# Expert and output products of 512 columns, and the last combine transposes moved into the output phase, in an attention and soft-MoE kernel on one core

## The chip, the cores and the metric

The kernel runs on one core of a Trainium2 chip. The core has a matrix engine (TensorE, PE in the profile), a vector engine (VectorE, DVE), an activation engine (ScalarE, ACT), a general engine (GpSimd, POOL) and a synchronising engine (SyncE, SP), and 16 DMA engines that move data between the chip's memory (HBM) and the on-chip buffer (SBUF). TensorE writes its products to PSUM, a small memory of eight banks; a bank holds 512 float32 columns on 128 partitions. The metric is device time in microseconds (us) of one launch.

## What is computed

The first half is chunk-selected attention. For 4 batches and 8 heads, sequence 768, head size 64, each query keeps 6 of 24 chunks of 32 keys, by an upper bound on the scores, and attends causally inside them. The second half is a soft mixture of experts on the result:

```python
x = attn_out.transpose(0, 2, 1, 3).reshape(B * S, H * D)      # 3072 x 512
logits = x @ phi                                              # 3072 x 32 (8 experts, 4 slots each)
d = np.exp(logits - logits.max(0, keepdims=True))
d /= d.sum(0, keepdims=True) + 1e-09                          # over all 3072 rows
slot_input = (d.T @ x).reshape(E, S_per_e, D)                 # 8 x 4 x 512
for e in range(E):
    h = np.maximum(slot_input[e] @ w1[e], 0.0)                # 512 -> 1024
    slot_out[e] = h @ w2[e]                                   # 1024 -> 512
c = np.exp(logits - logits.max(1, keepdims=True))
c /= c.sum(1, keepdims=True) + 1e-09                          # over the 32 slots of a row
out = c @ slot_out                                            # 3072 x 512
```

The inputs are float32; the loads turn them into bfloat16. The two weight tensors w1 and w2 are 16.8 MB each in float32, the output is 6.3 MB.

## The kernel before, in words

**Attention.** There are 16 steps, one for a pair of heads of one batch (4 steps for a batch). The order of the instructions on each engine is written out by hand. Each step does scores, exponentials, masks and the product with the values for its pair, and parts of the neighbours' work. The loads of k, q, v and of the 16 weight matrices (1 MB each in bfloat16, `load_w`, line 131) are issued by GpSimd, one queue, in a written order; `wplan` (line 518) says in which step a weight is asked for. The last one, the second matrix of the last expert, is asked for at the start of the last step, and its buffer takes the memory of tiles of earlier steps.

**The MoE part, batch by batch.** When a batch's four steps are through, its logits are made (`moe_logits`, line 389), the running column maximum is kept, the exponentials `d_sb` are taken, and `moe_dispatch` (line 478) multiplies them with x into the slot inputs; a fifth group of six products with a matrix of ones gives the column sums. Both are added to `si_acc`, which is rescaled when the maximum grows. `moe_ct` (line 495) transposes the row-wise exponentials `c_pad` of a batch on TensorE, six at a time, and VectorE copies them to `cT_all`.

**The last batch (lines 660 to 768)** does the same on a shorter way. Its logits are multiplied twice: once into `lg1`, from which the maxima are taken, and once into `lg2`, a PSUM tile to which a further product adds the negated maximum (line 720), so that ScalarE's exponential (line 728) reads it directly. `keep` issues unneeded products that keep TensorE busy.

**The experts (lines 771 to 859).** Eight experts with four slots each would leave most of the array empty; four experts are placed side by side, in four groups of 32 columns of the array. `experts_in` multiplies by w1, 512 columns at a time, for two halves f of the hidden size and two groups g of four experts; `relu` and `hidden_T` turn the result. `experts_out` (line 808) multiplies by w2 in two halves y of 256 columns, each in a PSUM tile and bank of its own, for the first seven experts. `last_expert_out(y)` (line 819) does the last expert, eight products for each half. `sums` (line 797) turns the slot sums into `zinv` and the last batch's row sums into `inv_b`, by one reciprocal. Behind the first half ScalarE scales by `zinv` (line 857), behind the second VectorE does (line 859); both write `so_sb`.

**The output (lines 861 to 889).** The 24 blocks of 128 rows go in 12 pairs, m = 0 to 11; a pair is 512 KB. The first pair is made in halves of 256 columns in four PSUM tiles and stored in three pieces (tile `first`). For the others two products of 256 columns fill a block, ScalarE scales the first block of a pair and VectorE the second, and SyncE issues the store (line 889; for the last pair block by block, line 887). There are five SBUF buffers for these pairs, so pair m = 5 waits until the first pair has been stored, and so on. The PSUM tiles come from three pools, `sc` and `tp` with two buffers and `at` with one.

Of the kernel before, what the change touches and what calls it, by code (L numbers as in the profile page):

```python
# [10 lines left out]
F32 = mybir.dt.float32  # L11
BF16 = mybir.dt.bfloat16
# [6 lines left out]
CH = 32  # L19
# [41 lines left out]
def kernel(  # L61
# [416 lines left out]
    def moe_dispatch(b):  # L478
        d_sb = st.pop(("d", b))
        x = st.pop(("x", b)).rearrange("p t h d -> p t (h d)").rearrange("p t (a c x) -> p t a x c", a=NDG // 2, x=2)  # L480
        si = p_tp.tile([P, NDG + 1, NS], F32, name="si_ps", tag="tp")
        for dg in range(NDG + 1):
            for t in range(NQT):
                nc.tensor.matmul(
                    si[:, dg, :], lhsT=x[:, t, dg // 2, dg % 2, :] if dg < NDG else ones_sq,
                    rhs=d_sb[:, t, :], start=(t == 0), stop=(t == NQT - 1),
                )
        if b == 0:
            nc.vector.tensor_copy(si_acc, si)
        elif b < B - 1:  # L490
            nc.vector.tensor_tensor(si_acc, si_acc, si, op=ALU.add)
        else:
            st["si"] = si
# [190 lines left out]
    lg2 = p_sc.tile([P, 2, 512], F32, name="lg2_ps", tag="sc")[:, 0, :NQT * NS].rearrange("p (t s) -> p t s", t=NQT)  # L684
    h_ps = [p_sc.tile([P, 2, 512], F32, name="h_ps0", tag="sc")]
    moe_logits(BL, range(NDG - 1), lg2, False)
# [19 lines left out]
    moe_logits(BL, range(NDG - 1, NDG), lg2, False)  # L706
# [6 lines left out]
    inv_b = tail.tile([P, 1 + NQT], F32, name="inv_b")  # L713

    def cinv(n):
        return inv_a[:, n:n + 1] if n < BL * NQT else inv_b[:, 1 + n - BL * NQT:2 + n - BL * NQT]

    keep(2)
    rep = identf[:NS, :NS].rearrange("p (o s) -> p o s", o=1)
    nc.tensor.matmul(  # L720
        lg2, lhsT=mneg.broadcast_to([NS, P]), rhs=rep.broadcast_to([NS, NQT, NS]), start=False, stop=True,
    )
# [4 lines left out]
    d_sb = small.tile([P, NQT, NS], BF16, name="d_sb", tag="d_sb")  # L727
    nc.scalar.activation(d_sb, lg2, func=ACT.Exp)
    st["d", BL] = d_sb
    rm = small.tile([P, NQT, 1], F32, name="rm", tag="rm")  # L730
    nc.vector.tensor_reduce(rm, lg1, axis=AX.X, op=ALU.max)
    nc.vector.reciprocal(inv_a, csa)
    dm = small.tile([P, 1, NS], F32, name="dm", tag="dm")
    nc.vector.tensor_tensor(dm[:, 0, :], m_old, bc, op=ALU.add)
# [3 lines left out]
    nc.vector.tensor_tensor(si_acc, si_acc, dm.broadcast_to([P, NDG + 1, NS]), op=ALU.mult)  # L738
    for g in range(2):
# [12 lines left out]
    for g in range(2):  # L752
# [4 lines left out]
            si[:, :NDG, sl].rearrange("p a (j s) -> p a j s", j=4), op=ALU.add,  # L757
        )
    for g in range(2):
# [4 lines left out]
            si[:1, NDG, sl].rearrange("p (j s) -> p j s", j=4), op=ALU.add,  # L764
# [3 lines left out]
    zinv = inv_b[:, :1]  # L768
# [3 lines left out]
    so_sb = [tail.tile([P, Dm // 2], BF16, name=f"so_sb{y}") for y in range(2)]  # L772
# [24 lines left out]
    def sums():  # L797
        ps = p_tp.tile([P, 1 + NQT], F32, name="z_ps", tag="tp")
        nc.tensor.matmul(
            ps[:, :1], lhsT=zrow.rearrange("p j s -> p (j s)"), rhs=identf[:1, :1], start=True, stop=True)  # L800
        col_sums(ps[:, 1:], BL)
        nc.vector.reciprocal(inv_b, ps)

    HD = Dm // 2
    so_t = p_at.tile([P, 2, 512], F32, name="so_ps0", tag="at")
    so_ps = [so_t[:, 0, :HD], p_sc.tile([P, HD], F32, name="so_ps1", tag="sc")]

    def experts_out(fs, es, ys):
        for y, f in ((y, f) for y in ys for f in fs):
            for fg in range(f * 4, (f + 1) * 4):  # L810
                for e in es:
                    g, j = divmod(e, 4)
                    nc.tensor.matmul(
                        so_ps[y][j * CH:(j + 1) * CH, :], lhsT=hT_pad[:, fg, e, :],
                        rhs=w_sb[E + e][:, fg * Dm + y * HD:fg * Dm + (y + 1) * HD],
                        start=(g == 0 and fg == 0), stop=False,
                    )

    def last_expert_out(y):
# [100 lines left out]
```

## Time and profile before

| what | value |
|---|---|
| median of 3 runs | 165.73 us (165.38 to 166.21) |
| the profiled execution, its own time | 166.11 us |
| its span, first to last instruction | 164.4 us |
| TensorE busy | 141.0 us (86%), 2541 products |
| VectorE busy | 121.8 us (74%) |
| ScalarE busy | 122.9 us (75%) |
| GpSimd busy | 103.0 us (63%) |
| read from HBM, written | 52.49 MB, 6.29 MB |

The profile shows one execution. A page of it gives the busy time of each engine, the span in 40 slices of 4.11 us, the chain of waits that ended last, the costliest groups of instructions and the DMA issues. Further views list instructions in order of time (timeline), who waited for whom, and the busy time of each engine in chosen windows. A row such as "PE L823 MATMUL so_ps<-w_sb,hT_pad 128*32 128x256 bf16 x16" means: TensorE, line 823, sixteen products into so_ps, each with a stationary operand of 128 by 32 and 256 moving columns. What stands in brackets behind a row is the idle time of the engine before it and what ended that. PEld is TensorE's weight load; SPq is SyncE's queue of issued DMAs.

### The profile page before, as it was taken

Reading aid. Unit: us, or ns where it says so; the run is one execution under the profiler, and the core shown is the slowest. Engines: PE = TensorE matmul, PEld = TensorE weight load, DVE = VectorE, ACT = ScalarE, POOL = GpSimd, SP = SyncE. Lnnn points to the kernel's source line nnn. Section 1 sums busy time; section 2 is a strip of 40 time slices with the busy share of each in tenths; the row PEclk is TensorE's granted clock in tenths of the full one; section 3 lists DMA queues with packets and bytes.
Section 4 is the critical chain, followed back from the end, with each engine's and each line's share of the span. In section 5 each row is a group of like instructions: output and inputs, shape, how many; then the busy total and the mean of one; then the engine's idle time right before and its main releaser. Section 6 shows DMA issues by size and latency. Waiting matters only on the chain.

```text
span 164.4 us, 6143 instructions
## 1 busy us (share of the span) xinstructions
PE 141.0 (86%) x2541; PEld 97.3 (59%) x2541; DVE 121.8 (74%) x424; ACT 122.9 (75%) x168; POOL 103.0 (63%) x203
## 2 busy tenths in 40 slices
PE   7696779999999999999999899998989999494600
PEld 2253356766777686676777567775768748372300
DVE  4466989999999989999997999899526521175530
ACT  3759879999999898999898899997886311183530
POOL 6988759989889398888949896768937100000000
PEclk9999999999999999999999999999999999959755
DMA  3999999999999999999999999999999999159994
GB/s 48 137 134 166 203 184 135 174 191 203 201 201 205 202 204 182 211 196 177 211 189 215 194 213 193 210 219 195 206 209 212 211 217 197 34 198 370 405 408 157
DMA packets 40604, 32.94 MB, mean 200 GB/s; under 512 B 26368, under 2 KB 34816, under 8 KB 40576
## 3 DMA queue, kind: packets, MB, share of 16 engines
q0 software_dynamic: 38416, 26.25, 108.5%
q1 hardware_dynamic: 2160, 6.29, 9.8%
q8 instruction: 20, 0.33, 0.8%
q14 instruction: 8, 0.07, 0.1%
HBM read 52.49 MB, written 6.29 MB: 358 GB/s over the span
## 4 chain that ended last, share of the span: by engine, by line
PE 36%; DMA 24%; ACT 14%; DVE 11%; issue 6%; POOL 4%; DVEq 0%; POOLq 0%; ACTq 0%; SPq 0%
DMA w_sb<-in_moe_w_dram 15%; ACT e_sb L325 10%; PE sc_ps L301 7%; DMA out_dram<-o_sb 6%; PE at_ps L353 6%; PE sc_ps L311 5%; PE tr_ps L209 5%; ACT qT L218 3%; PE xT_ps L375 3%; DMA k_in<-in_k_dram 3%; PE ub_ps L260 2%; DVE x_sb L366 2%; DVE mx L272 2%; DVE qpn L243 1%; PE ub_ps L253 1%
## 5 line engine op out<-in xcount | busy, mean ns | idle before, releaser
L325 ACT ACTIVATE e_sb<-sc_ps 128x1024 bf16<-128x1024 f32 (+1 forms) x96 | 83.2, 917 | 7.7 <-PE sc_ps L311 7.2
L335 POOL TENSOR_SCALAR_AFFINE_SELECT e_sb<-e_sb 128x256 bf16<-128x256 bf16 x96 | 38.4, 418 | 16.2 <-ACT e_sb L325 15.7
L301 PE MATMUL sc_ps<-qT,kT 64*128 64x384 bf16 (+3 forms) x258 | 36.8, 305 | 2.7 <-ACT e_sb L325 1.9
L311 PE MATMUL sc_ps<-nsT,smask 64*128 64x384 bf16 (+2 forms) x294 | 38.2, 284 | 0.1
L353 PE MATMUL at_ps<-v_t,e_sb 128*128 128x65 bf16 x672 | 29.7, 194 | 1.2 <-DVE x_sb L366 1.0
L353 PEld LDWEIGHTS <-e_sb 128*128 128x128 bf16 x672 | 25.5, 98 | 3.5 <-issue 1.9
L301 PEld LDWEIGHTS <-kT 64*128 64x128 bf16 x258 | 14.0, 93 | 10.9 <-issue 5.4
L272 DVE MAX8 mx<-ub_ps 128x8 f32<-128x8 f32 (+1 forms) x192 | 16.8, 162 | 3.8 <-PE ub_ps L260 2.9
L311 PEld LDWEIGHTS <-smask 64*128 64x128 bf16 x294 | 15.0, 94 | 3.8 <-issue 0.6
L151 POOL DMA_DIRECT2D v_t<-in_v_dram x16 | 16.6, 1039 | 0.6 <-PE ns_ps L283 0.5
L227 DVE TENSOR_REDUCE mm<-kT 128x24 bf16<-128x768 bf16 x16 | 15.1, 943 | 2.2 <-ACT kT L218 2.2
L366 DVE TENSOR_TENSOR x_sb<-at_ps,inv 128x768 bf16<-128x768 f32 (+1 forms) x17 | 15.5, 910 | 0.6
L233 DVE TENSOR_REDUCE mm<-kT 128x24 bf16<-128x768 bf16 x16 | 15.1, 942 | 0.0
L218 ACT COPY qT<-tr_ps 128x768 bf16<-128x768 bf16 x16 | 12.8, 799 | 2.3 <-PE tr_ps L209 2.3
L218 ACT COPY kT<-tr_ps 128x768 bf16<-128x768 bf16 x16 | 12.9, 804 | 1.0 <-PE tr_ps L209 1.0
L146 POOL DMA_DIRECT2D k_in<-in_k_dram x16 | 11.7, 734 | 1.1 <-POOLq L904 0.8
L146 POOL DMA_DIRECT2D q_in<-in_q_dram x16 | 11.5, 720 | 0.0
L139 POOL DMA_DIRECT2D w_sb<-in_moe_w_dram x16 | 11.4, 716 | 0.0
L882 PE MATMUL o_ps<-so_sb,cT_all 128*128 128x256 bf16 x44 | 8.0, 332 | 3.7 <-ACT o_sb L844 3.6
L386 DVE COPY xT_sb<-xT_ps 128x768 bf16<-128x768 bf16 (+1 forms) x15 | 8.0, 537 | 3.2 <-PE xT_ps L375 3.2
L209 PE MATMUL tr_ps<-ident,k_in 128*64 128x128 bf16 x192 | 8.4, 223 | 0.9 <-DMA k_in<-in_k_dram 0.8
L247 DVE TENSOR_SCALAR qpn<-qT 128x768 bf16<-128x768 bf16 x15 | 9.1, 607 | 0.0
(131 smaller groups left out, 210.3 us busy)
## 6 DMA issues: line engine op xcount, KB each, us to landing
w_sb<-in_moe_w_dram POOLq DMA_DIRECT2D x16, 1024.0 KB, 13.4
out_dram<-o_sb SPq DMA_DIRECT2D x10, 512.0 KB, 5.2
k_in<-in_k_dram POOLq DMA_DIRECT2D x16, 192.0 KB, 6.8
q_in<-in_q_dram POOLq DMA_DIRECT2D x16, 192.0 KB, 7.1
v_t<-in_v_dram POOLq DMA_DIRECT2D x16, 192.0 KB, 8.4
out_dram<-o_sb SPq DMA_DIRECT2D x2, 256.0 KB, 4.8
out_dram<-first SPq DMA_DIRECT2D x2, 128.0 KB, 2.0
out_dram<-first SPq DMA_DIRECT2D x1, 256.0 KB, 2.3
```

The source lines that it names most:

```text
L146: nc.gpsimd.dma_start(out=t, in_=src.rearrange("h (p g) d -> p h (g d)", p=P))
L151: nc.gpsimd.dma_start(out=v_t[i % NV][:, :, :, :D], in_=v[b, 2 * j:2 * j + 2].rearrange("h (g p) d -> p h g d", p=P),)
L209: nc.tensor.matmul(ps[h * 64:(h + 1) * 64, g, :], lhsT=src[:, h, g * D:(g + 1) * D], rhs=ident, is_transpose=True,)
L218: nc.scalar.copy(t.rearrange("d (p g) -> d p g", g=NQT), st.pop((nm + "ps", i)).rearrange("d g p -> d p g"),)
L227: nc.vector.tensor_reduce(mm[:, 0, 0, :], kT, axis=AX.X, op=ALU.min)
L272: nc.vector.max(mx[:, a, :], ub[:, a, :max(8, 4 * t + 4)])
L301: nc.tensor.matmul(ps[:, h, c:c + w], lhsT=kT[r, kg * P:(kg + 1) * P], rhs=qT[r, qs], start=True, stop=False,)
L311: nc.tensor.matmul(ps[:, h, c + (f - t0) * P:c + (l - t0) * P], lhsT=smask[r, x, kg].rearrange("p a b -> p (a b)"), rhs=nsT[r, (f - x * NJ ...
L325: nc.scalar.activation(e[:, :, :w], st.pop(("scps", i, g))[:, :, :w], func=ACT.Exp, scale=scale)
L335: nc.gpsimd.affine_select(out=e[:, :, c:c + P], in_=e[:, :, c:c + P], compare_op=ALU.is_ge, fill=0.0, base=0, pattern=[[0, 2], [1, P]], ch ...
L353: nc.tensor.matmul(o, lhsT=st["e", i, g][:, h, c:c + P], rhs=v_t[i % NV][:, h, kg, :], start=(kg == 0), stop=(kg == t),)
L366: nc.vector.tensor_tensor(st["x", b][:, t0:t1, 2 * j:2 * j + 2, :].rearrange("p t h d -> p h t d"), at[:, :, :, :D], inv.broadcast_to([P, ...
```

## The change

It has five parts.

1. `moe_dispatch`: the ones product runs once with 192 columns instead of six times with 32; VectorE then sums over the six row blocks (`z`) and adds the sum to `si_acc`.
2. The last batch's logits are made once. VectorE copies the broadcast negated maximum to SBUF (`bc_sb`), adds it to the logits (`ld`), and ScalarE's exponential reads `ld`. The reciprocal of the other batches' row sums moves behind the scaling of `si_acc`.
3. The second expert products go over 512 columns into one PSUM tile `so_ps`; `last_expert_out` runs once, and both halves are scaled behind it, the first by ScalarE and the second by VectorE, into one tile `so_all`.
4. An output block is one product of 512 columns. The order of the PSUM pools changes: ("at", "tp", "sc", "tp", "sc") for ("sc", "tp", "tp", "sc", "at"), and for the first pair ("sc", "sc") for ("sc", "at").
5. `moe_ct` of the last batch, its column sums and their reciprocal leave the expert phase (`last_rows`) and come behind pair m = 3 in the output loop. `slot_sums` keeps the part for `zinv`.

```diff
     def moe_dispatch(b):
...
-        si = p_tp.tile([P, NDG + 1, NS], F32, name="si_ps", tag="tp")
-        for dg in range(NDG + 1):
+        ps = p_tp.tile([P, (NDG + NQT) * NS], F32, name="si_ps", tag="tp")
+        si = ps[:, :NDG * NS].rearrange("p (a s) -> p a s", a=NDG)
+        zt = ps[:, NDG * NS:].rearrange("p (t s) -> p t s", t=NQT)
+        for dg in range(NDG):
...
+        nc.tensor.matmul(zt, lhsT=ones_sq, rhs=d_sb, start=True, stop=True)
...
+        z = small.tile([P, NS], F32, name="z", tag="z")
+        nc.vector.tensor_reduce(z, zt.rearrange("p t s -> p s t"), axis=AX.X, op=ALU.add)
+        if b == 0:
+            nc.vector.tensor_copy(si_acc[:, NDG, :], z)
         else:
-            st["si"] = si
+            nc.vector.tensor_tensor(si_acc[:, NDG, :], si_acc[:, NDG, :], z, op=ALU.add)
...
-    moe_logits(BL, range(NDG - 1), lg2, False)
...
-    moe_logits(BL, range(NDG - 1, NDG), lg2, False)
...
-    nc.tensor.matmul(
-        lg2, lhsT=mneg.broadcast_to([NS, P]), rhs=rep.broadcast_to([NS, NQT, NS]), start=False, stop=True,
-    )
...
-    nc.scalar.activation(d_sb, lg2, func=ACT.Exp)
...
+    nc.vector.tensor_copy(bc_sb[:, 0, :], bc)
+    ld = small.tile([P, NQT, NS], F32, name="ld", tag="ld")
+    nc.vector.tensor_tensor(ld, lg1, bc_sb.broadcast_to([P, NQT, NS]), op=ALU.add)
+    d_sb = small.tile([P, NQT, NS], BF16, name="d_sb", tag="d_sb")
+    nc.scalar.activation(d_sb, ld, func=ACT.Exp)
...
-    def sums():
-        ps = p_tp.tile([P, 1 + NQT], F32, name="z_ps", tag="tp")
-        nc.tensor.matmul(
-            ps[:, :1], lhsT=zrow.rearrange("p j s -> p (j s)"), rhs=identf[:1, :1], start=True, stop=True)
-        col_sums(ps[:, 1:], BL)
-        nc.vector.reciprocal(inv_b, ps)
+    def slot_sums():
+        ps = p_tp.tile([P, 1], F32, name="z_ps", tag="tp")
+        nc.tensor.matmul(ps, lhsT=zrow.rearrange("p j s -> p (j s)"), rhs=identf[:1, :1], start=True, stop=True)
+        nc.vector.reciprocal(zinv, ps)
+
+    def last_rows():
+        moe_ct(BL)
+        ps = p_tp.tile([P, NQT], F32, name="cs_ps", tag="tp")
+        col_sums(ps, BL)
+        nc.vector.reciprocal(inv_b, ps)
...
-    so_t = p_at.tile([P, 2, 512], F32, name="so_ps0", tag="at")
-    so_ps = [so_t[:, 0, :HD], p_sc.tile([P, HD], F32, name="so_ps1", tag="sc")]
+    so_ps = p_at.tile([P, 2, 512], F32, name="so_ps0", tag="at")[:, 0, :]
...
-    moe_ct(B - 1)
...
-    experts_out([0, 1], [4, 5, 6], [0, 1])
-    last_expert_out(0)
-    nc.scalar.activation(so_sb[0], so_ps[0], func=ACT.Copy, scale=zinv)
-    last_expert_out(1)
-    nc.vector.tensor_scalar_mul(so_sb[1], so_ps[1], zinv)
+    experts_out([0, 1], [4, 5, 6])
+    last_expert_out()
+    nc.scalar.activation(so_sb[0], so_ps[:, :HD], func=ACT.Copy, scale=zinv)
+    nc.vector.tensor_scalar_mul(so_sb[1], so_ps[:, HD:], zinv)
...
-            tag = ("sc", "tp", "tp", "sc", "at")[n % 5]
+            tag = ("at", "tp", "sc", "tp", "sc")[n % 5]
             o_ps = homes[tag].tile([P, Dm], F32, name="o_ps", tag=tag)
-            for y in range(2):
-                nc.tensor.matmul(
-                    o_ps[:, y * HD:(y + 1) * HD], lhsT=cT[:, m, x], rhs=so_sb[y], start=True, stop=True)
+            nc.tensor.matmul(o_ps, lhsT=cT[:, m, x], rhs=so_all, start=True, stop=True)
...
         if m < NM - 1:
             nc.sync.dma_start(out=rows(m), in_=o_sb)
+        if m == 3:
+            last_rows()
```

More of the change, by code (lines that the diff above doesn't have):

```diff
@@ L738 @@
     nc.vector.tensor_tensor(si_acc, si_acc, dm.broadcast_to([P, NDG + 1, NS]), op=ALU.mult)
+    nc.vector.reciprocal(inv_a, csa)
     for g in range(2):
@@ L767 @@
         zrow[:, :, 2 * SPE:3 * SPE], zrow[:, 3:4, SPE:2 * SPE].broadcast_to([1, 4, SPE]))
[L768 removed]
     cT = cT_all.rearrange("p (m a) (c x) -> p m x (a c)", a=2, x=2)
     h_sb = tail.tile([P, 2, 512], BF16, name="h_sb")
[L772 removed]
+    so_all = tail.tile([P, Dm], BF16, name="so_all")
+    so_sb = [so_all[:, y * Dm // 2:(y + 1) * Dm // 2] for y in range(2)]
     h_ps.append(p_sc.tile([P, 2, 512], F32, name="h_ps1", tag="sc"))
```

63 lines of the change are left out of this document (32 added, 31 removed).

## The prediction

> **What bounds the kernel now.** I read the page first, for the stages; then the chain of waits from 110 us on; then the rows of the weight loads, the timeline and the windows of the last 24 us.
>
> ```profile
> PEclk9999999999999999999999999999999999959755
> DMA  3999999999999999999999999999999999159994
> GB/s 48 137 134 166 203 184 135 174 191 203 201 201 205 202 204 182 211 196 177 211 189 215 194 213 193 210 219 195 206 209 212 211 217 197 34 198 370 405 408 157
> ```
>
> From the second slice to the 34th the DMA engines are never under nine tenths busy, at 135 to 219 GB/s; then comes one almost empty slice (34 GB/s), then the output at 370 to 408 GB/s. The granted clock falls right behind that hole.
>
> ```profile
> 118.10 24.61 DMA w_sb<-in_moe_w_dram
> ...
> 142.75 0.43 PE so_ps L823 x8
> ...
> 143.73 0.98 PE oh_ps L866 x4
> 144.71 1.29 PE o_ps L882 x6
> ```
>
> The last weight (the last expert's second matrix) is issued at 118.10 and lands 24.61 us later, behind the loads before it. Its landing starts the last chain: eight products, then (with ScalarE's scaling between) the first output products. The rows of that stretch:
>
> ```profile
> 142.75 0.62 PE L823 MATMUL so_ps<-w_sb,hT_pad 128*32 128x256 bf16 x16 [1.87 <-DMA w_sb<-in_moe_w_dram]
> 143.20 0.47 ACT L857 ACTIVATE so_sb<-so_ps,inv_b 128x256 bf16<-128x256 f32 x1 [6.17 <-PE so_ps L823]
> 143.42 0.48 DVE L859 TENSOR_SCALAR so_sb<-so_ps,inv_b 128x256 bf16<-128x256 f32 x1 [5.03 <-PE so_ps L823]
> 144.29 0.42 PE L866 MATMUL oh_ps<-so_sb,cT_all 128*128 128x256 bf16 x1
> 144.50 0.42 PE L882 MATMUL o_ps<-so_sb,cT_all 128*128 128x256 bf16 x1
> 144.53 0.88 DVE L847 TENSOR_SCALAR first<-oh_ps,inv_a 128x256 f32<-128x256 f32 x2 [0.63 <-PE oh_ps L866]
> ```
>
> TensorE had waited 1.87 us for that weight. So what is taken away ahead of 142.75 buys nothing while the landing stays, and what is added there is free up to 1.87 us. From 142.75 on, delay counts in full as long as the stores run back to back afterwards:
>
> ```profile
> 143.79:147.20 3.41, 3.41 (x17) 2.45 (x17) 2.49 (x5) 2.53 (x5) 0.00 (x0) 0.50 0.43 151
> 147.20:150.60 3.40, 2.48 (x19) 1.67 (x18) 2.07 (x4) 1.62 (x3) 0.00 (x0) 1.00 0.92 360
> 150.60:154.00 3.40, 1.19 (x8) 0.78 (x8) 1.84 (x3) 1.73 (x3) 0.00 (x0) 1.00 1.01 402
> ```
>
> The last three columns are granted clock, DMA share and GB/s. From 147.2 the stores run at 360 to 402 GB/s: the rest of the kernel is a fixed number of bytes, moved by whatever delays its start. The granted clock is 0.50 for 3.41 us after the hole.
>
> **The change, part by part.** *Ahead of the landing.*
>
> ```profile
> 126.81 0.60 PE L395 MATMUL lg_ps<-phi_sb,xT_sb 128*128 128x32 bf16 x18
> 128.32 0.36 DVE L705 TENSOR_REDUCE pm<-lgt_ps 128x32 f32<-128x192 f32 x1 [0.34 <-PE lgt_ps L395]
> 129.38 0.59 PE L720 MATMUL lg_ps<-identf,mb 32*128 32x192 f32 x2
> 130.07 0.33 ACT L728 ACTIVATE d_sb<-lg_ps 128x192 bf16<-128x192 f32 x1 [2.59 <-PE lg_ps L720]
> 130.15 0.19 DVE L734 TENSOR_TENSOR dm<-m_run,bc_ps 128x32 f32<-128x32 f32 x1 [0.35 <-PE bc_ps L724]
> 130.25 0.35 DVE L737 TENSOR_TENSOR lc<-lgt_ps,rm 128x192 f32<-128x192 f32 x1
> 131.06 0.30 PE L484 MATMUL si_ps<-d_sb,ones_sq 128*128 128x32 bf16 x6
> 131.73 1.05 PE L779 MATMUL h_ps<-w_sb,siT_pad 128*32 128x512 bf16 x16
> 132.71 0.51 PE L498 MATMUL cT_ps<-ident,c_pad 128*128 128x128 bf16 x6
> 137.85 0.30 PE L692 MATMUL z_ps<-live,cT_all 128*128 128x1 bf16 x6
> 138.08 2.80 PE L813 MATMUL so_ps<-w_sb,hT_pad 128*32 128x256 bf16 x80
> ```
>
> Removed: the second copy of the logits (18 products in 0.60 us here, six more behind the last head, and the 0.59 us product with the negated maximum). In their place VectorE copies the 32 bounds (near the 0.19 us of the add at 130.15) and adds them to 192 columns (0.35 us, as lc). ScalarE's exponential then waits for VectorE instead of TensorE; dm, lc and the scaling of si_acc stand behind the new add on VectorE. The removed products stand ahead of the last head's transposes, which then start some 0.3 us earlier (an estimate: half of the 0.60), the two VectorE steps and their handovers put about 0.4 us back: between 0.3 us earlier and 0.5 later, I take 0.1 later. The slot sums lose five of six weight loads and products (at most 0.30 us) and gain a 192-column product; in the three earlier batches VectorE gains a 192-to-32 reduction and a 128x32 copy or add, about 0.5 us each time (0.36 as the reduction of pm, 0.19 as the small add). The last combine transposes (0.51 us) and their column sums (0.30) leave this stage. The second expert products become 56 with 512 columns for 112 with 256. Eighty of these take 2.80 us, 35 ns each; the 16 of 512 columns at 131.73 take 1.05 us, 66 ns each, about twice as much: no gain, give or take 0.3 us. Together TensorE is through about 0.8 us sooner (0.5 later to 1.5 sooner), and all of it disappears in the wait for the weight, which grows from 1.87 to some 2.7 us. If the cover were gone, the worst end, three times 0.5 on VectorE plus 0.5, would just use it up: 2.0 against 1.87 plus the 0.8 taken away. The load itself gains one wait on TensorE for memory it reuses, the buffers of an earlier step; it is issued 24.6 us ahead behind a full queue, so a delay of microseconds there leaves the landing. Cost: nothing.
>
> *The split of the last expert.* Today ScalarE starts after 8 of the 16 products, at 143.20. With eight of 512 columns there is no first half: the same columns take the same 0.62 us, and ScalarE starts when VectorE does today, 143.42: **+0.22 us**. Bounds: 0, or 0.43 were the products half clocked.
>
> *Two readers of one bank.* so_ps is now one 512-column tile. In the changed program VectorE's scaling waits for ScalarE's alone, though they read different halves. So VectorE starts at 143.42 + 0.47 + 0.05 = 143.94 instead of 143.42 and ends at 144.43. Behind it on VectorE stand the two pieces of `first`, and TensorE waits for it with the second-half products. The first two products start at 143.95 and 144.16 and no longer hold the third up; the third starts at 144.48, the fourth 0.21 later at 144.69, against 144.29 now: **+0.40 us** in all for everything behind, the 0.22 included, and 0.41 for VectorE's first piece (144.53 now, 144.94). Bounds: 0.22, if the halves overlapped after all, and 0.53, if all waited for VectorE.
>
> The Trainium skill ("PSUM — Partial Sum Buffer", section "PSUM bank collisions raise a hardware error") says that ScalarE and VectorE must not read one bank at once even in different columns, and that dependencies are put between them. By that rule the wait can't be scheduled away and the term is 0.40; without it 0.22. The rows at 143.20 and 143.42, which overlap, are of two different banks, so no run here yet shows it.
>
> *Output products of 512 columns.*
>
> ```profile
> L882 PEld LDWEIGHTS <-cT_all x44: 96/98/152, 144.3 to 155.6; 128*128 128x128 bf16 x44
> L882 PE MATMUL o_ps<-so_sb,cT_all x44: 269/273/421, 144.5 to 155.8; 128*128 128x256 bf16 x44
> ```
>
> Six of them took 1.29 us in the chain at half clock, 0.215 each, while the duration of one is 0.42: starts follow the columns, and one product of 512 columns takes as long as two of 256. The weight loads of 0.15 us lie beside that. Nothing from this; the far end, where each of the first blocks saves a weight load, is a rival below.
>
> *The last transposes among the stores.* They come after the fourth pair of row blocks (m = 3).
>
> ```profile
> L506 DVE COPY cT_all<-cT_ps x4: 543/547/558, 62.0 to 133.3; 128x768 bf16<-128x768 bf16 x4
> L802 DVE RECIPROCAL inv_b<-z_ps x1: 205/205/205, 138.2 to 138.2; 128x7 f32<-128x7 f32 x1
> 145.50:146.00 0.50, 0.50 (x5) 0.32 (x4) 0.40 (x1) 0.36 (x1) 0.00 (x0) 0.50 0.78 260
> 147.31 0.75 DVE L847 TENSOR_SCALAR o_sb<-o_ps,inv_a 128x512 f32<-128x512 f32 x1
> 144.65 0.84 SPq L872 DMA_DIRECT2D out_dram<-first  x2
> 148.13 1.51 SPq L889 DMA_DIRECT2D out_dram<-o_sb  x1
> 149.74 0.39 SPq L889 DMA_DIRECT2D out_dram<-o_sb  x1
> ```
>
> VectorE scales m = 3 until 148.06, so 148.46 in the new time; then copies the transposes (0.55), TensorE sums columns (0.30), VectorE inverts (0.20) and scales m = 4 (0.75), with handovers of 0.05 (ScalarE's end at 143.67, TensorE's start at 143.73): m = 4 is ready at 150.46. On TensorE the products of m = 4 stand behind the column sums, on VectorE its scaling behind the reciprocal. Now SyncE issues that store at 149.74, because the store before it kept SyncE for 1.51 us; then at about 150.5. Is that too late? By 150.60 the windows moved 151 x 3.41 + 360 x 3.40 = 1.74 MB of the 2.10 MB issued before m = 4, so these run out near 151.5 now, 151.9 then. From issue to bytes the first store took about 0.9 us (144.65; by 146.00 the half microsecond from 145.5 is 0.78 busy). 150.5 + 0.9 = 151.4: in time by 0.5 us. Cost: nothing, at most 1.26 us (0.55 + 0.30 + 0.20 + 0.20) if the whole insertion shows.
>
> **Sum:** 0 + 0.40 + 0 + 0 = +0.4 us. The profiled execution took 166.11 us (span 164.4 and 1.7 around it): 166.5. It lies 0.38 above the median of 165.73, whose runs spread from 165.38 to 166.21. On the median: **166.1 us**.
>
> **The rivals.**
>
> *Stores run dry (slower).* The mechanism is the insertion at m = 3; it decides once m = 4 is issued later than about 151.0. For it: only 0.5 us of cover, and SyncE's unexplained 1.51 us hold, which could fall on the fourth store instead; half clock would add up to 0.3 us to the transposes and sums. Against: m = 4 was scaled by about 148.8 (148.06 + 0.75) and waited 0.9 us for SyncE today, and the buffers for m = 5 come free as now. Price 0.2 to 1.2 us, say 0.7: 166.8 us.
>
> *A colder clock (slower).* The hole grows from 1.87 to about 2.7 us, and the window 143.79 to 147.20 shows half clock in one piece of 3.41 us after a hole. If such a piece starts before 142.75, the eight products take about 0.43 us longer, but it also ends earlier. Price 0 to 0.43: 166.1 to 166.5 us. The Trainium skill ("TensorE: Matmul & The Clock Gate", Part 1) says that the window is free-running, 3413 ns long, so where it falls differs between runs; by it this case comes and goes from run to run, which three runs of one kernel without a longer hole can't show.
>
> *Hidden (same).* If the stores' end were set by something that doesn't move with their start, as the 1.51 us hold, nothing is lost: 165.7 us. Against it: 360 to 402 GB/s until the end.
>
> *Faster.* If half clock rather than the columns set the pace of the output, each of the first six row blocks would save a weight load (0.15 us at half clock in the trace): 0.4 - 0.9 = -0.5, so 165.2; and with the hole over at full clock a little under 164.9. Against: 0.215 us from start to start is the columns alone.
>
> That the change does not do what it says can be left out: the changed program holds 64 second products and 22 output products of 512 columns.
>
> **How the numbers follow.** Forecast 0.46; stores run dry 0.26; colder clock 0.12; hidden 0.10; faster 0.06. About 0.5% (0.83 us, 164.9 to 166.56) is what a measurement of this kernel can tell from no change. Within it lie the forecast but for 0.02, the hidden case, half of the cold one and none but the smallest starvation: 0.60; above: 0.34; below: 0.06. The range goes from the lowest run with nothing lost, 165.3, to 166.1 with the far end of a starved store, 167.3.
>
> **What would show it.** Right: the wait for the weight at the last expert's products grows beyond 1.87 us while the weight lands at the same time; ScalarE and VectorE scale so_sb one after the other; the first o_sb store is issued 0.4 us later after the landing; DMA share stays at nine tenths or more around 151 us. Wrong: the weight lands at another time, VectorE's scaling overlaps ScalarE's, a hole in the GB/s around 151 us, or a granted clock of 0.50 already at the last expert's products.

## The result, and the profile after

| | before | after |
|---|---|---|
| median of 20 runs each, side by side | 166.42 us (164.84 to 167.59) | 166.95 us (166.10 to 168.43) |
| ratio after / before, 95% interval | | 1.0066 [1.0041, 1.0091] |
| profiled execution, its span | 166.11, 164.4 | 166.54, 164.8 |
| TensorE busy, products | 141.0, 2541 | 140.1, 2408 |

The kernel became slower by 0.66% by the ratio, about 1.1 us. The ratio leaves out runs that are over 1.5% above the fastest of their kernel, and the medians of all 20 differ by only 0.53 us, so the size of the loss is less certain than the interval says. The forecast was +0.4 us, as a difference that could not be told from no change; the interval excludes no change. Run together once more, below, the ratio was 1.0049 [1.0013, 1.0084].

The page of the changed kernel, the rows that were read first before. Each digit is one of 40 slices of 4.12 us:

```profile
PEclk9999999999999999999999999999999969999955
DMA  3999998999999999999999999999999999058994
GB/s 47 148 144 169 209 175 103 182 198 203 201 204 201 203 203 181 211 191 182 214 188 216 188 214 190 215 215 199 203 207 216 212 216 191 18 190 343 406 409 186
```

Two things differ. The granted clock now falls in slice 33 (131.8 to 136.0 us), in the middle of the expert products and ahead of the hole in the transfers, where before it fell behind it. And the output has a weaker slice of its own (343, DMA 8) and a fuller last one (186 for 157).

The chain of waits of the changed kernel, from the last batch's logits on (shortened):

```profile
126.69 0.57 PE lgt_ps L395 x16
...
131.18 0.33 DVE si_acc L746
131.74 0.56 PE h_ps L689 x2
...
133.87 3.85 PE h_ps L790 x47
...
138.06 0.98 PE h_ps L790 x16
139.04 0.86 PE so_ps L826 x16
...
140.56 2.32 PE so_ps L826 x34
143.09 0.68 PE so_ps L835
143.79 0.48 ACT so_all L867
...
146.76 4.70 DMA out_dram<-o_sb
```

What is missing is the 24.61 us line of the last weight's transfer. Before, the chain went through that transfer; now it goes through steps of several engines until 131.7, the reciprocal last among them, and from there to 143.8 through TensorE's own work without a break. The views of TensorE's waits from 139 to 145 us say the same (waiter, releaser, us in all, times, longest). Before:

```profile
PE so_ps L823 <- DMA w_sb<-in_moe_w_dram: 1.9, 1, 1.9
PE oh_ps L866 <- ACT so_sb L857: 0.4, 1, 0.4
```

After:

```profile
PE oh_ps L875 <- ACT so_all L867: 0.6, 1, 0.6
```

The wait that was to grow from 1.87 to 2.7 us is gone. The timeline of the changed kernel shows the end of the expert products, and the scaling behind it:

```profile
142.50 0.39 PE L835 MATMUL so_ps<-w_sb,hT_pad 128*32 128x512 bf16 x1
...
142.92 0.39 PE L826 MATMUL so_ps<-w_sb,hT_pad 128*32 128x512 bf16 x3
143.13 0.60 PE L835 MATMUL so_ps<-w_sb,hT_pad 128*32 128x512 bf16 x6
...
143.79 0.47 ACT L867 ACTIVATE so_all<-so_ps,zinv 128x256 bf16<-128x256 f32 x1 [4.10 <-PE so_ps L835]
144.30 0.48 DVE L868 TENSOR_SCALAR so_all<-so_ps,zinv 128x256 bf16<-128x256 f32 x1 [3.54 <-ACT so_all L867]
```

L835 is the last expert, L826 the others. By the trace the weight lands 23.0 us behind its issue at 118.57, so at 141.56; its last load packet ends at 141.24. The first product that needs it starts only at 142.50, and at 143.13 TensorE is still at other experts' products: the eight end at 143.73. Before, they ended 0.66 us behind the landing (142.71 and 143.37), which would be 142.22 here. So TensorE is **1.5 us late** behind a weight that landed 1.15 us earlier than before; the products end 0.36 us later. Then the two scalings run one behind the other, as forecast.

Where TensorE lost its time, in the timeline of the changed kernel:

```profile
130.66 0.36 ACT L739 ACTIVATE d_sb<-ld 128x192 bf16<-128x192 f32 x1 [2.71 <-DVE ld L737]
...
131.42 0.26 DVE L747 RECIPROCAL inv_a<-h_ps 128x18 f32<-128x18 f32 x1
131.74 0.56 PE L689 MATMUL h_ps<-w_sb,ident 128*128 128x480 bf16 x2 [1.80 <-DVE inv_a L747]
...
132.14 0.76 PE L486 MATMUL si_ps<-d_sb,x_sb 128*128 128x32 bf16 x24
```

The exponentials `d_sb` are ready at 131.02. The slot inputs' products (L486), which need them, start at 132.14: ahead of them in TensorE's order stand two of the unneeded products that keep it busy (`keep`, L689), and those wait 1.80 us for the reciprocal of the other batches' row sums (L747). Both use one PSUM tile: the row sums lie in columns 0 to 17 of half 1 of `h_ps[0]`, the unneeded products go to columns 32 to 511 of the same half. In part 2 of the change this reciprocal moved behind the scaling of `si_acc`. Before, the same products started at 130.46, 0.06 us behind the exponentials' end at 130.40:

```profile
130.04 0.58 PE L678 MATMUL h_ps<-w_sb,ident 128*128 128x480 bf16 x2
130.46 0.76 PE L484 MATMUL si_ps<-d_sb,x_sb 128*128 128x32 bf16 x24
```

Windows of 3.41 us, laid along the edges of the granted clock (us, then busy time of TensorE, its loads, VectorE, ScalarE, GpSimd, then granted clock, DMA share, GB/s), after:

```profile
129.33:132.74 3.41, 1.61 (x30) 1.18 (x29) 1.83 (x8) 1.00 (x5) 0.00 (x0) 1.00 1.05 211
132.74:136.16 3.42, 3.42 (x34) 1.20 (x33) 0.86 (x5) 0.00 (x0) 0.19 (x1) 0.50 1.05 211
```

and before:

```profile
129.33:132.74 3.41, 3.41 (x56) 2.04 (x56) 1.75 (x9) 1.19 (x5) 0.19 (x1) 1.00 1.06 214
132.74:136.16 3.42, 3.42 (x62) 1.78 (x62) 0.85 (x3) 0.60 (x1) 0.00 (x0) 1.00 1.08 218
```

With the wait TensorE is busy for only 1.61 us of the first window, and the next one is granted half the clock: 34 products for 62. The dispatch is 1.7 us later than before. Of this 0.47 us stood there already at the last normalisation of attention (`x_sb`, 126.78 for 126.31) and 0.15 us comes from the new steps to the exponentials; the other 1.1 us are the moved 0.26 us reciprocal, which holds the products back from 131.08 to 132.14. Half the clock over 3.42 us costs up to 1.7 us more, and the cover ahead of the weight is used up.

### The profile page after: what moved, and what is told of

It reads as the page before. It is cut to its first block, busy times and chain, and to the rows that moved or that the text cites. A ratio compares the mean times of both kernels' runs of the same rounds, so it can differ in the third digit from the quotient of the medians.

```text
span 164.8 us, 5869 instructions
## 1 busy us (share of the span) xinstructions
PE 140.1 (85%) x2408; PEld 91.7 (56%) x2409; DVE 123.2 (75%) x434; ACT 122.8 (74%) x168; POOL 103.2 (63%) x203
## 4 chain that ended last, share of the span: by engine, by line
PE 41%; DVE 22%; ACT 14%; DMA 9%; issue 6%; POOL 4%; DVEq 0%; POOLq 0%; ACTq 0%; SPq 0%
ACT e_sb L325 9%; PE sc_ps L301 7%; DMA out_dram<-o_sb 6%; PE at_ps L353 6%; PE sc_ps L311 5%; PE tr_ps L209 4%; PE xT_ps L375 3%; DVE mx L272 3%; PE h_ps L790 3%; DVE x_sb L366 3%; DMA k_in<-in_k_dram 3%; ACT qT L218 2%; DVE mm L233 2%; DVE mm L227 2%; PE so_ps L826 2%
## 5 line engine op out<-in xcount | busy, mean ns | idle before, releaser
L335 POOL TENSOR_SCALAR_AFFINE_SELECT e_sb<-e_sb 128x256 bf16<-128x256 bf16 x96 | 38.5, 418 | 16.1 <-ACT e_sb L325 15.4
L301 PEld LDWEIGHTS <-kT 64*128 64x128 bf16 x258 | 13.9, 93 | 10.6 <-issue 5.3
L272 DVE MAX8 mx<-ub_ps 128x8 f32<-128x8 f32 (+1 forms) x192 | 16.9, 163 | 3.8 <-PE ub_ps L260 2.9
L890 PE MATMUL o_ps<-so_all,cT_all 128*128 128x512 bf16 x21 | 6.0, 377 | 3.3 <-ACT o_sb L854 3.1
```

What stands on the lines that cost most here:

```text
L272: nc.vector.max(mx[:, a, :], ub[:, a, :max(8, 4 * t + 4)])
L301: nc.tensor.matmul(ps[:, h, c:c + w], lhsT=kT[r, kg * P:(kg + 1) * P], rhs=qT[r, qs], start=True, stop=False,)
L335: nc.gpsimd.affine_select(out=e[:, :, c:c + P], in_=e[:, :, c:c + P], compare_op=ALU.is_ge, fill=0.0, base=0, pattern=[[0, 2], [1, P]], ch ...
```

## The experiments

The theory after these traces, **R**: the moved reciprocal makes TensorE last, and that is most of the loss. The rivals: **S**, the split and the one bank, as forecast, are all of it (0.36 us from the traces, 0.2%); **T**, the transposes in the output phase starve the stores; **F**, something in the output phase itself, where SyncE's hold was unexplained. Times are ratios to the kernel before in runs on the same chip, with 95% intervals, beside its median there (165.92 us in the first series of runs, 166.07, 165.91 and 166.02 in the others).

**The reciprocal alone, taken back and put in.** In the changed kernel, back to its old place:

```diff
     nc.vector.tensor_reduce(rm, lg1, axis=AX.X, op=ALU.max)
+    nc.vector.reciprocal(inv_a, csa)
     bc_sb = small.tile([P, 1, NS], F32, name="bc_sb", tag="bc_sb")
...
     nc.vector.tensor_tensor(si_acc, si_acc, dm.broadcast_to([P, NDG + 1, NS]), op=ALU.mult)
-    nc.vector.reciprocal(inv_a, csa)
     for g in range(2):
```

> The changed kernel with one line moved back: the reciprocal of the other batches' row sums stands ahead of the copy of the bounds on VectorE again. Theory R (reciprocal): in the changed kernel TensorE's keep-busy products wait 1.8 us for that reciprocal, because the sums lie in the PSUM tile they write to; the dispatch is late by 1 us and the half clock falls on the expert products. Then this run is 0.6 us below the changed kernel (0.3 to 1.0), the wait of TensorE at the keep-busy products is under 0.3 us, and TensorE waits again for the last weight. Theory S (split): the loss lies behind the landing, in one bank read by two engines; then this run is within 0.2 us of the changed kernel.

Measured: 1.0026 [0.9979, 1.0072], 165.73 us: 0.4% under the changed kernel's 1.0066, with intervals that overlap. The wait for the reciprocal is gone, and TensorE waits for the weight again, 0.57 us.

```profile
131.15 0.36 ACT L740 ACTIVATE d_sb<-ld 128x192 bf16<-128x192 f32 x1 [2.70 <-DVE dm L743]
131.56 0.77 PE L486 MATMUL si_ps<-d_sb,x_sb 128*128 128x32 bf16 x24 [0.51 <-ACT d_sb L740]
```

In this execution the half clock fell in the expert phase all the same (132.11 to 135.52). The reverse, the kernel before with nothing but the reciprocal moved to behind the scaling of `si_acc`:

```diff
     nc.vector.tensor_reduce(rm, lg1, axis=AX.X, op=ALU.max)
-    nc.vector.reciprocal(inv_a, csa)
     dm = small.tile([P, 1, NS], F32, name="dm", tag="dm")
...
     nc.vector.tensor_tensor(si_acc, si_acc, dm.broadcast_to([P, NDG + 1, NS]), op=ALU.mult)
+    nc.vector.reciprocal(inv_a, csa)
     for g in range(2):
```

> The kernel before with only the reciprocal moved behind the scaling of si_acc, as the change has it. Theory R: the keep-busy products wait more than 0.7 us, the dispatch starts 0.8 us later, and the kernel is 0.3 to 1.0 us slower than before, more than the 1.87 us of slack would allow, because the longer hole brings the half clock into the expert products. Theory S: within 0.2 us of the kernel before.

Measured: 1.0102 [1.0052, 1.0152], 167.05 us. This one line, put into the old kernel, costs about as much as the whole change, and more than the 0.3 to 1.0 us expected. TensorE waits 1.21 us for it, the expert phase gets its half clock, and the wait for the weight is gone. R is shown as a mechanism that costs time by itself. Its price can't be read from this one trace: here the weight landed 0.9 us later than in the kernel before (143.60 for 142.71), just as TensorE came to it.

**The halves alone.** In the changed kernel, part 3 undone: two PSUM tiles of 256 columns, `last_expert_out` twice, ScalarE's scaling behind the first half.

```diff
-    last_expert_out()
-    nc.scalar.activation(so_sb[0], so_ps[:, :HD], func=ACT.Copy, scale=zinv)
-    nc.vector.tensor_scalar_mul(so_sb[1], so_ps[:, HD:], zinv)
+    last_expert_out(0)
+    nc.scalar.activation(so_sb[0], so_ps[0], func=ACT.Copy, scale=zinv)
+    last_expert_out(1)
+    nc.vector.tensor_scalar_mul(so_sb[1], so_ps[1], zinv)
```

> The changed kernel with the second expert products in two halves of 256 columns and two banks again; output products stay at 512 columns. Theory S: 0.4 us below the changed kernel (0.2 to 0.6), the two scalings overlap again. Theory R: the scalings overlap, but the start of the stores is set by the late expert products; the gain is still about 0.2 to 0.4 us, since these two steps are behind them in the chain, and the 1.8 us wait at the keep-busy products stays.

> The changed kernel with only the halves back, once more, as the partner of the next run in one call: the two differ in one line, the place of the reciprocal, and in both the fetch comes ahead of the stores. Theory R: 0.6 to 1.5 us above the next run, TensorE late for the last weight. If the reciprocal is hidden: within 0.3 us of it.

Measured: 1.0005 [0.9966, 1.0044], 165.25 us, and the same kernel again 0.9947 [0.9905, 0.9990], 165.19 us: about 0.6% to 1.2% better than the changed kernel, more than S's 0.36 us. Its trace in the second run:

```profile
143.65 0.69 PE L838 MATMUL so_ps<-w_sb,hT_pad 128*32 128x256 bf16 x14
144.18 0.47 ACT L871 ACTIVATE so_all<-so_ps,zinv 128x256 bf16<-128x256 f32 x1 [3.93 <-PE so_ps L838]
144.40 0.48 DVE L873 TENSOR_SCALAR so_all<-so_ps,zinv 128x256 bf16<-128x256 f32 x1 [3.06 <-PE so_ps L838]
...
147.01 1.89 SPq L901 DMA_DIRECT2D out_dram<-o_sb  x3
```

From the end of the last product (143.65 + 0.69 = 144.34) to the first whole store (147.01) it takes 2.67 us, against 143.73 to 146.76 = 3.03 us in the changed kernel: S is 0.36 us in the trace. The rest of this gain goes with F, below: the 64 products more also moved a fetch.

**The last transposes alone.** In the changed kernel, part 5 undone: `moe_ct` and the column sums back in the expert phase.

```diff
     experts_in(0, 0)
+    moe_ct(BL)
...
     slot_sums()
+    last_rows()
...
-        if m == 3:
-            last_rows()
```

> The changed kernel with the last transposes and their column sums in the expert phase again. Theory T (stores run dry): the hole in the stores near 149 us goes, 0.5 us below the changed kernel. Theory R: TensorE is last before the output in the changed kernel, so the 0.8 us of work put back ahead of it makes it 0.3 to 0.8 us slower than the changed kernel; the hole near 149 us belongs to SyncE's long issue and stays.

Measured: 1.0068 [1.0030, 1.0105], 166.28 us, the same as the changed kernel (1.0066); theory R's 0.3 to 0.8 us did not show either. This run decides nothing by itself: its edit also moved the fetch of the next experiment ahead of the stores, which last 16.48 us in its trace for 17.47, while TensorE is 2.3 us late for the weight. T is settled by the last experiment.

**A count of instructions, nothing else.** The trace's DMA records hold a queue that the page lists as q8, "instruction": TensorE's own program, fetched in blocks of 16,384 bytes, one about every 256 of its instructions (20 blocks for 5,082 products and weight loads before). One of these blocks falls among the stores in both kernels. In the changed kernel, DMA transfers between 147.0 and 148.8 us (queue, kind: packets, MB, share of the 16 engines):

```profile
q1 hardware_dynamic: 245, 0.67, 95.8%
q8 instruction: 1, 0.02, 5.5%
```

5.5% of 16 engines over 1.8 us is 1.6 us on one engine; the record starts at 147.11. SyncE's issue of the second whole store, in the window from 147.3 on, lasts through that:

```profile
147.41 1.68 SPq L896 DMA_DIRECT2D out_dram<-o_sb  x1
```

and before, with a record at 147.56, it is the row at 148.13 that the prediction called unexplained (1.51 us). So a few dozen tiny products of eight columns, put in the first microseconds, shift the fetch to ahead of the stores without touching anything else; 18 of them in the changed kernel (six in each of three places, one of which is shown), 25 in the kernel before, and 18 in the changed kernel with its reciprocal back:

```diff
+    def tiny(n):
+        for _ in range(n):
+            nc.tensor.matmul(warm_ps[:, 0, :8], lhsT=ones_sq, rhs=ones_sq[:, :8], start=True, stop=True)
     warm(9)
+    tiny(6)
     transposes(0, "k")
```

> The changed kernel with 18 tiny products (36 instructions) more on TensorE in the waits for the first loads. They move nothing at the end but the place in TensorE's program where its next 16 KB of instructions are fetched: in the changed kernel that fetch runs among the stores, from 147.1, for 1.6 us instead of 0.9, and holds one DMA engine. Theory F (fetch): moved ahead of the stores, to about 142.7, it takes the long SyncE issue and the hole in the stores away: 1.2 us below the changed kernel (0.7 to 1.5), stores' length 16.1 us for 17.5. Theory T (the insertion at m = 3 runs the stores dry): the hole stays and the time is within 0.2 us of the changed kernel.

> The changed kernel once more, unaltered, beside the others of this call: 1.1 us above the kernel before (0.6 to 1.6) by all theories.

> The kernel before with 25 such tiny products (50 instructions), which move its fetch from 147.6 to about 142.8. Theory F: 1.2 us below the kernel before (0.7 to 1.5), since that kernel has the fetch among its stores as well; the 1.51 us issue of its third o_sb store goes. Theory T: no difference, within 0.2 us.

> The changed kernel with the reciprocal back at its place and the 18 tiny products. Theories R and F together: 0.6 us for the reciprocal and 1.2 us for the fetch, 1.8 us below the changed kernel and 0.7 below the kernel before. Theory R without F: 0.6 below the changed kernel. Theory S alone: as the changed kernel.

Measured: changed kernel shifted 0.9993 [0.9952, 1.0033], 165.78 us; unshifted beside it 1.0049 [1.0013, 1.0084], 166.94 us, so 0.6% between the ratios, 1.2 us by the medians. The kernel before shifted 0.9990 [0.9950, 1.0029]: no gain that can be told from none, where 1.2 us were expected. The changed kernel with its reciprocal back, shifted: 0.9969 [0.9928, 1.0010], 165.73 us; that is 0.2% below the shifted changed kernel, within the noise. Windows of the output, changed kernel (last two columns: DMA share, GB/s):

```profile
146.00:149.00 3.00, 1.69 (x18) 0.88 (x16) 2.60 (x6) 1.36 (x3) 0.00 (x0) 1.00 0.93 340
149.00:152.00 3.00, 1.96 (x8) 0.68 (x7) 1.97 (x4) 1.81 (x3) 0.00 (x0) 1.00 0.83 328
```

and shifted:

```profile
146.00:149.00 3.00, 1.71 (x14) 0.83 (x14) 2.34 (x6) 1.27 (x3) 0.00 (x0) 1.00 1.03 406
149.00:152.00 3.00, 2.14 (x8) 0.60 (x7) 2.33 (x4) 1.91 (x4) 0.00 (x0) 1.00 1.02 401
```

The hole around 149 us is not there in the shifted kernel, though the transposes stand among the stores in both. By the DMA records the stores last 17.47 us from first to last packet in the changed kernel and 17.59 before, 16.59 and 16.58 in the two shifted kernels. The hole and the long issue are not what makes the difference: in the unshifted run beside them the fetch came at 148.12, the window from 149 on is full (396 GB/s), no issue took over 1.22 us, and the stores still took 17.66 us, 1.3 us of it for the last 0.04 MB. F costs about 1 us in the traces, but the kernel before pays it as well: it hides or adds time in the experiments (a kernel with a few TensorE instructions more or less can gain it) and is not the cause of the difference. That the runs of the shifted old kernel don't show this 1 us stays open.

**Both undone, and one put in.** The changed kernel with the first two edits together (the reciprocal and the halves back; run twice), and the old kernel with part 3 only (its hunks of the change, and the order of the PSUM pools that they need):

```diff
-    last_expert_out(0)
-    nc.scalar.activation(so_sb[0], so_ps[0], func=ACT.Copy, scale=zinv)
-    last_expert_out(1)
-    nc.vector.tensor_scalar_mul(so_sb[1], so_ps[1], zinv)
+    last_expert_out()
+    nc.scalar.activation(so_sb[0], so_ps[:, :HD], func=ACT.Copy, scale=zinv)
+    nc.vector.tensor_scalar_mul(so_sb[1], so_ps[:, HD:], zinv)
```

> The changed kernel with both undone: the reciprocal at its old place and the second expert products in two halves and two banks. TensorE's program is as long as in the run with the halves alone, so its fetch should again come ahead of the stores. Theories R, S and F together: 1.0 to 2.0 us below the changed kernel, 0.3 to 1.0 below the kernel before, and 0 to 0.5 below the run with the halves alone; TensorE waits for the last weight again. If the reciprocal is worth nothing, as that run.

> The changed kernel with the halves and the reciprocal back. Theory R: 0.6 to 1.5 us below the run before it and 1.0 to 2.0 below the kernel before; TensorE waits for the last weight by 0.5 us or more.

> The kernel before with only the second expert products in one 512-column tile, scaled by two engines behind each other (output products stay at two of 256). It has 128 TensorE instructions fewer, so the fetch that fell among the stores should come near 141 to 143. Theory S: from the end of the last product to the first whole o_sb store 3.0 us at full clock, 0.36 more than in two halves (2.67); in all 0.36 for the split against about 1.0 for the fetch: 0.6 us below the kernel before. If the fetch is worth nothing: 0.4 above.

Measured: 0.9882 [0.9829, 0.9935], 164.26 us (6 runs), again 0.9895 [0.9851, 0.9939], 164.02 us; the old kernel with one bank 0.9896 [0.9832, 0.9959], 164.90 us (6 runs), so faster although S went into it: it has 64 products fewer, and its fetch falls at 140.58, ahead of the stores. The fetch need not be all of that, since the shift alone gave the old kernel 0.1%; what else it is wasn't tested. The second run of the first kernel beside the halves alone (0.9947) is R by itself with the fetch ahead of the stores in both (141.34 and 142.56): 1.2 us between the medians (165.19 and 164.02), 0.5% between the ratios, whose intervals overlap. The rows of that second run:

```profile
130.15 0.56 PE L689 MATMUL h_ps<-w_sb,ident 128*128 128x480 bf16 x2
131.22 0.75 PE L486 MATMUL si_ps<-d_sb,x_sb 128*128 128x32 bf16 x24 [0.50 <-ACT d_sb L740]
...
132.43 0.83 PE L790 MATMUL h_ps<-w_sb,siT_pad 128*32 128x512 bf16 x12
```

and at the end, where TensorE again waits for the weight:

```profile
141.96 0.62 PE L838 MATMUL so_ps<-w_sb,hT_pad 128*32 128x256 bf16 x16 [1.12 <-DMA w_sb<-in_moe_w_dram]
142.41 0.47 ACT L871 ACTIVATE so_all<-so_ps,zinv 128x256 bf16<-128x256 f32 x1 [5.23 <-PE so_ps L838]
142.63 0.48 DVE L873 TENSOR_SCALAR so_all<-so_ps,zinv 128x256 bf16<-128x256 f32 x1 [4.36 <-PE so_ps L838]
```

**The wait or the clock.** Two kernels ask which half of R costs: the changed kernel without the two unneeded products ahead of the dispatch, and the one with both undone with six of them in place of two:

```diff
     spread_c(lc)
-    keep(2)
     moe_dispatch(BL)
```

> The changed kernel with the reciprocal late as it is, but without the pair of keep-busy products between the broadcast of the maximum and the dispatch. Theory R: what hurts is not the reciprocal but what waits for it ahead of the dispatch on TensorE; without it the dispatch starts 1 us earlier (at d_sb's exponential, not at the reciprocal) and the time is 0.3 to 0.8 us below the changed kernel, like the run with the reciprocal back. If the delay of the dispatch is hidden anyway: as the changed kernel, within 0.2 us.

```diff
     spread_c(lc)
-    keep(2)
+    keep(6)
     moe_dispatch(BL)
```

> As the run before it, with six keep-busy products instead of two ahead of the dispatch. If the half clock in the expert phase comes from TensorE's short waits around 128 to 132, it is gone, TensorE is ready over 1.5 us earlier and waits for the weight longer; the time stays within 0.3 us, because the weight is last, or grows by up to 0.4 if the longer wait brings the half clock to the output products.

Measured: 1.0014 [0.9970, 1.0059], 166.72 us without them: the dispatch no longer waits for the reciprocal, but the clock is at half from 129.8 to 136.6, and the weight is not waited for. With six, 0.9901 [0.9866, 0.9937], 163.98 us, the time of the kernel with two (164.02): no half clock in the expert phase, but one from 143.95 on, in the output. The profile of the kernel with two had none in the expert phase either, so this pair doesn't price the clock. Other traces give a size. From the start of the last normalisation to the end of the other experts' products TensorE takes 13.9 us with both undone (no half clock), 15.4 with the reciprocal back (half clock), and 16.0 to 16.5 in the three profiles of the changed kernel, the shifted one among them. So, as an estimate, the half clock costs 1.5 us and the wait 0.6 to 1.1. The clock isn't the reciprocal's alone: it can fall without it.

**The transposes once more**: the edit of the third experiment (`moe_ct` and `last_rows` in the expert phase) on top of the reciprocal and the halves taken back:

> The changed kernel with the reciprocal, the halves and the last transposes back, which leaves of the change the dispatch, the logits once and the output products of 512 columns. If the transposes among the stores cost nothing and buy nothing while the weight is last: within 0.3 us of the run with reciprocal and halves back; if their 0.8 us on TensorE counts after all: 0.3 to 0.8 above it.

Measured: 0.9894 [0.9846, 0.9942], 163.81 us (6 runs), against 0.9895 with the transposes in the output phase. In both traces the fetch falls ahead of the stores (141.12 and 141.34), which last 16.16 and 16.10 us: T is nothing.

**Fifteen traces together.** What TensorE does at the last weight, and whether half clock fell on the expert products. "Late" is the end of the last expert's products beyond 0.66 us behind the landing:

| profiles | reciprocal | at the last weight | half clock |
|---|---|---|---|
| kernel before; shifted; with one bank | early | waits 1.9, 1.2, 2.3 us | in none |
| changed, reciprocal back; both back (second run); six products | early | waits 0.6, 1.1, 1.6 us | in the first |
| both and the transposes back | early | neither waits nor late | yes |
| changed; again; shifted; no pair; transposes back | late | late 1.5, 1.0, 0.3, 0.8, 2.3 us | in all |
| halves back, twice | late | late 0.0, 1.5 us | in both |
| kernel before, reciprocal late | late | late 0.2 us | yes |

With the late reciprocal TensorE never waits for the weight and is 0.9 us late in the mean of eight; with the early one it is never late.

The best versions, 0.988 to 0.990, are parts 1, 2, 4 and 5 without the moved reciprocal and without the one bank (one of them without part 5): about 1.1% faster than the kernel before, about 1.7% faster than the changed one. Their stores last 16.1 us, 17.6 before, with the fetch ahead of them, so how much of the 1.1% belongs to these parts isn't separated.

## Why the prediction was wrong, point by point

- **"Ahead of the landing … Cost: nothing": wrong, and this is the step that failed.** It counted the two VectorE steps and their handovers and took "0.1 later". That term was right: 0.15 us in the traces. But it put the moved reciprocal at nothing without a word, though the change lists it, and nothing in it asks who waits to write where that reciprocal reads. The reciprocal alone held the dispatch back by 1.1 us, outside the bounds given (0.5 later). The half clock that followed came on top; the prediction's colder clock was placed at the last eight products and priced at 0 to 0.43 us, not in the expert phase. Together they used up the cover, and the end moved from the weight to TensorE, 1.5 us late in the profiled execution. The runs price the reciprocal at +1.0% [0.5, 1.5] in the old kernel; in the new one three pairs say 0.4%, 0.2% and 0.5%, all of one sign, none clear of noise by itself.
- **The wait for the weight grows to 2.7 us: wrong**; it fell to none. It was the first of the signs listed, and the first row to look at. The landing was not the same either: it came 1.15 us earlier.
- **Split and one bank, +0.40: right in mechanism and near in size.** 0.36 us in the traces up to the first whole store; the two scalings run one behind the other in one bank (143.79 and 144.30) and overlap in two (144.18 and 144.40). The rule of the Trainium skill ("PSUM — Partial Sum Buffer", section "PSUM bank collisions raise a hardware error") agrees with these rows: two column ranges of one bank, and VectorE waits for ScalarE.
- **512-column output products, nothing: right as far as seen.** In the changed kernel the store of m = 1 is issued 2.97 us behind ScalarE's start, before 3.23 us; that difference goes with the clock, which was at half there before and is full now. No run tests this part alone. With two banks and the fetch ahead of the stores these last 16.10 us with products of 512 columns (both undone) and 16.58 with two of 256 (the shifted old kernel); the cause of that difference, which lies in the last 0.04 MB, is open.
- **Transposes among the stores, nothing: right**, from the pair with the fetch ahead of the stores in both (0.9894 for 0.9895). Of the rival "stores run dry" a hole came true in the first profile, but not by the insertion, which comes behind m = 3: SyncE's hold, which the prediction had named as a way to it, fell on the second whole store (the row at 147.41) and delayed m = 3. In the second profile of the same kernel there was none.
- **SyncE's 1.51 us hold: goes with the fetch** of TensorE's program beside the stores; with the fetch moved ahead that issue of the old kernel takes 0.75 us. It does not come with every such fetch. "Hidden" and "faster" did not happen.

The sum of the two profiled executions: TensorE late 1.5 us, the landing 1.15 us earlier, 0.17 us more from the products' end to the first stored packet (one bank, less the half clock that was there before), stores 0.12 us shorter: +0.4 us, and the spans differ by 0.43. That the profiled execution came out at 166.54 us, where 166.5 was forecast for it, is luck: an early landing hid most of a cost that the sum did not have. From the traces, 0.9 us of mean lateness and 0.36 us for the one bank make about 1.3 us (an estimate); the 20 runs of each say 1.1 us by the ratio (0.7 to 1.5) and 0.5 by the medians. The landing of the last weight lies anywhere from 141.2 to 143.6 us in the fifteen traces, so no single pair of profiles gives the size.

## What to carry to other kernels

When an instruction moves, look up not only who needs its result but who is waiting for its operands' memory: here filler products in a PSUM tile that a late reader still held stopped TensorE for 1.8 us. Cover in front of a late transfer (0 to 2.3 us here, from one trace to the next) is spent by the sum of several small delays and by the clock they take away, so add all of them up before anything is called hidden. When two profiles agree with a sum, look at each of its terms: here a landing that happened to be early made up for one that was missing. And when two builds differ by a few dozen instructions, look at the program fetches in the DMA records before a difference of one microsecond is given to the change.

## What was unexpected in the hardware

- **The program fetch competes with the stores.** A block of 16 KB mostly takes 0.9 to 1.0 us on one DMA engine among the loads, and 0.95 to 1.6 us among the stores. In some of these profiles SyncE's store issue is long meanwhile (1.68 us after, 1.51 before); in all, the stores last 17.4 to 17.7 us for 16.1 to 16.9. The Trainium skill ("Runtime: NRT & Kernel Launch", section "Instruction fetch mechanics") describes blocks of this size, fetched by each engine over a queue of its own, and calls their cost mostly hidden. The size agrees with the records here; the cost was hidden only where the fetch fell ahead of the stores. How much a shift is worth isn't settled: 0.6% in the changed kernel, 0.1% ± 0.4 in the kernel before.
- **Half clock after a short wait.** A window in which TensorE was busy for 1.61 of 3.41 us was followed by one at a granted clock of 0.50, with no wait longer than 1.80 us in it; in the kernel with the reciprocal back it came with a longest wait of 0.51 us. Where it falls differs between profiles of one kernel: 3.41 us from 132.75 and from 131.93 in the changed kernel, 3.41 us from 132.24 and 6.83 us from 130.31 with the halves back. The kernel with the reciprocal back:

```profile
128.70:132.11 3.41, 2.54 (x36) 1.59 (x35) 2.34 (x9) 0.96 (x5) 0.37 (x2) 1.00 1.07 216
132.11:135.52 3.41, 3.41 (x36) 1.24 (x36) 0.86 (x5) 0.04 (x1) 0.19 (x1) 0.50 1.07 216
```
